# A decode attention kernel: TensorE's loop step reordered to keys, last chunk, maximum, values, with the last chunk of the last pair ahead of the values of the pair before it

## The chip, the cores and the metric

The kernel runs on one core of one Trainium2 chip. The metric is the device time of one execution in microseconds (us). Before the change three runs gave 1269.72, 1269.49 and 1268.3 us, so the median is 1269.49 us. The profiled execution, from which all durations below come, took 1268.6 us, and its span from the first to the last instruction is 1266.8 us.

## The reference

One new token is attended against a cache of 65,536 positions, and the result is mixed with a small token MLP. The parts that matter:

```python
q = (x @ wq)                     # 16 query heads of 256, 8 key/value heads, so 2 query heads per cache head
scores = einsum("bhqd,bhkd->bhqk", q, k) * (Dh ** -0.5)     # k_cache: 8 x 65536 x 256 bf16
p = softmax(scores, axis=-1)
a = einsum("bhqk,bhkd->bhqd", p, v).reshape(1, 1, 4096) @ wo   # v_cache: 8 x 65536 x 256 bf16
b = mixer(layernorm(x), w1, b1, w2, b2)                     # gelu, 1792 wide
return g * a + (1 - g) * b                                  # g = sigmoid(sum(x * gate_w))
```

Both caches are read once, 537 MB together; everything else is small.

## The kernel before

**Tiling.** A cache head has 65,536 positions. A *chunk* is 2,048 positions (16 tiles of 128), a *pair* is 8 chunks (`BODY = 8`), so a pair of one cache is 8.39 MB. There are 32 pairs (`NP = 32`), four to a head (`PPH = 4`). Pairs and chunks count from 0 here; the argument of `values(v)` counts from 1, so `values(31)` works on pair 30.

**What is done to a pair.** For each chunk TensorE transposes 16 key tiles into PSUM (`transposes`, L335, the matmuls at L348), VectorE and ScalarE copy them to SBUF (`ktT<-kst`, L681 and L821), and TensorE multiplies them with the head's two queries (`scores`, L360, the matmuls at L369). A chunk's scores are issued one step behind its transposes. `keys` (L375) does the transposes of chunks 0 to 6 and the scores of chunks 0 to 5; `last_keys` (L382) does the transposes of chunk 7 and the scores of chunks 6 and 7. Then the running maximum is updated: VectorE reduces the scores (L687, L690), TensorE transposes the result (L390), VectorE reduces again (L692, L694), TensorE broadcasts it (L392), VectorE rescales the accumulators (L697 to L710, semaphore `s_acc`), ScalarE forms the weights `pT`. `values` (L408) then sums the denominators (L397) and multiplies `pT` with the 128 value tiles in `vbuf` (L404).

**Buffers.** `kring` holds one and a half pairs of keys, `vbuf` one pair of values.

**The DMA order.** All large loads stand on SyncE's (SP's) queue in a fixed order (L283 to L316). The load of key pair j waits until TensorE has transposed chunk 3 of pair j-1 (L288, `sem_tr`). The load of value pair j waits until the values of pair j-1 are done (L276, `sem_pv`). The last value pair, pair 31, comes in five pieces (L68, L305): tiles 0 to 47 go into `kring` once all keys of pair 30 are transposed; tiles 48 to 95, 96 to 111, 112 to 123 and 124 to 127 go into `vbuf` and wait for `sem_pv` 31, that is for the values of pair 30. The last two loads of the projection weights `wo` (L314) stand behind them.

**TensorE's loop.** The order of work on TensorE is made at run time: a loop of 35 passes (L540) over parts guarded by conditions on register counters. `k_reg`, `l_reg` and `v_reg` count the pairs whose keys, last chunk and values have been issued. In each pass come `keys` (if `k < cap`), `values` (if `v < l`), then in one condition (`l < k`) the last chunk, the head's end (`clear`, `by_row`, `project`), the mixer's product, `maxima` and, for the last pair, `first_of_last` (L424), and at the very end `tail` (L477). Followed by hand, the registers give: pairs 0 and 1 run keys, last chunk, maximum, values one pair after the other; pair 2 stops after its maximum; from pair 3 on the order is keys j, values j-1, last chunk j, maximum j. The order at the end is keys 31, values of pair 30, last chunk 31, maximum 31, `first_of_last` (the first 48 value tiles of pair 31), the rest of its values, `tail`.

**The wait `s_qc`.** VectorE copies the two queries of the next head into `qcur` after the maximum of the head's last pair (L744, L767) and increments `s_qc`; TensorE waits for it ahead of each pair's keys (L546).

**The end.** `first_of_last` waits for `s_acc`, for the weights and for `s_mix` (VectorE's L771 to L774). `values(32)` waits for the pieces of tiles 48 to 95 and 96 to 111. `tail` waits for VectorE's copy of the accumulators (`accs`, L715), transposes them (L452), adds the last 16 tiles (L445), waits for VectorE's `oTn` (L728) and projects with `wo` (L471).

Of the kernel before, what the change touches and what calls it, by code (L numbers as in the profile page):

```python
# [12 lines left out]
def bass_gated_mix__gqa_block_cached__mixer_token_mlp__decode_kernel(  # L13
# [17 lines left out]
    H = A_k_cache.shape[1]  # L31
# [4 lines left out]
    REP = HQ // H  # L36
# [59 lines left out]
    with ctx:  # L96
# [6 lines left out]
        def new_sem(name):  # L103
            return ctx.enter_context(nc.semaphore(name))
# [91 lines left out]
        sem_k = new_sem("sem_k")  # L196
        sem_kb = new_sem("sem_kb")
        sem_kc = [new_sem("sem_kc%d" % i) for i in range(3)]
        s_qc = new_sem("s_qc")
        sem_v = new_sem("sem_v")  # L200
        sem_vp = [new_sem("semvp%d" % i) for i in range(len(pieces))]
        sem_x = new_sem("sem_x")
# [128 lines left out]
        def _(pe):  # L331
# [3 lines left out]
            def transposes(k, c, j, u16, x2):  # L335
                if k == 0:
                    pe.wait_ge(sem_k, u16)
                if k == DC:
                    pe.wait_ge(sem_kb, 16)
                    for p, sem in zip((LEAD, LEAD + 1, NP - 1), sem_kc):  # L340
                        with pe.If(j == p):
                            pe.wait_ge(sem, 16)

                def tiles(at):
                    for b in range(NB):
                        pe.wait_ge(sem_ev[b], c + 1)
                        for i in range(4):
                            ins = pe.transpose(kst[:, b, i * P:(i + 1) * P],  # L348
                                               kring_f[:, at + NT * (k % DC) + 4 * b + i, :], ident[:, :])
                        ins.then_inc(sem_tr[b], 1)  # L350

                if k < DC:
                    tiles(HV)
                else:
                    with pe.If(x2 == 0):
                        tiles(0)
                    with pe.Else():
                        tiles(NV)
# [16 lines left out]
            def keys(c0, j, *where):  # L375
                j1 = pe.snap(j + 1, min_val=1, max_val=NP)
                transposes(0, c0, j, *where)
                for k in range(1, BODY - 1):
                    transposes(k, c0 + k, j, *where)
                    scores(k - 1, c0 + k - 1, j1)  # L380
# [19 lines left out]
            def some(n0, n1, buf):  # L400
                for n in range(n0, n1):
                    r, nt = divmod(n, NT)
                    o = 32 * (n % 4)
                    ins = pe.matmul(acc[o:o + REP, 0:DH], pT[:, r, 2 * nt:2 * nt + 2], buf[:, n, :],  # L404
                                    start=False, stop=False, skip_group_check=True)
                return ins

            def values(v):  # L408
                pe.wait_ge(s_acc, v)
                pe.wait_ge(sem_exp, pe.snap(v + 1, min_val=2, max_val=NP + 1))  # L410
                denominators()
                with pe.If(v < NP):
                    pe.wait_ge(sem_v, pe.snap(v * 16, min_val=16, max_val=16 * NP))
                    some(0, NRING, vbuf)
                for n0, n1 in pieces[1:]:
                    if n0 < NLATE:
                        with pe.If(v == NP):
                            piece_wait(n0)
                        ins = some(n0, n1, vbuf)
                ins.then_inc(s_early, 1)  # L420
                with pe.If(v < NP):
                    some(NLATE, NV, vbuf).then_inc(sem_pv, 1)

            def first_of_last():  # L424
                pe.wait_ge(s_acc, NP)
# [94 lines left out]
            def reg(name, value):  # L520
                r = pe.alloc_register(name)
                pe.reg_mov(r, value)
                return r
# [3 lines left out]
            k_reg = reg("k_reg", 0)  # L527
            l_reg = reg("l_reg", 0)
            v_reg = reg("v_reg", 0)
            cap_reg = reg("cap_reg", 1)  # L530
            mk_reg = reg("mk_reg", 0)
            gk_reg = reg("gk_reg", 1)
            mv_reg = reg("mv_reg", 0)
            gv_reg = reg("gv_reg", 1)
            mix_reg = reg("mix_reg", 1)
            def val(r, lo=0, hi=NP):
                return pe.snap(r, min_val=lo, max_val=hi)

            on = OrderedEngineSet([pe.engine])
            with nc.Fori(0, NP + LEAD + 1, 1, engines=on, head_slot={pe.engine: 0}):  # L540
                with pe.If(val(k_reg) < val(cap_reg)):
                    j = pe.snap(k_reg, min_val=0, max_val=NP - 1)
                    with pe.If(val(mk_reg) == PPH):
                        pe.reg_mov(mk_reg, 0)
                        pe.reg_add(gk_reg, gk_reg, 1)
                    pe.wait_ge(s_qc, pe.snap(gk_reg, min_val=1, max_val=H))  # L546
                    keys(pe.snap(j * BODY, min_val=0, max_val=NC), j,
                         pe.snap(j * 16 + 16, min_val=16, max_val=16 * NP),
                         pe.snap(x2_reg, min_val=0, max_val=NV))
                    pe.reg_sub(x2_reg, NV, x2_reg)  # L550
                    pe.reg_add(k_reg, k_reg, 1)
                    pe.reg_add(mk_reg, mk_reg, 1)
                with pe.If(val(v_reg) < val(l_reg)):
                    pe.reg_add(v_reg, v_reg, 1)
                    pe.reg_add(mv_reg, mv_reg, 1)
                    pe.reg_add(cap_reg, v_reg, 1)
                    v = pe.snap(v_reg, min_val=1, max_val=NP)
                    values(v)
                    with pe.If(v >= LEAD):
                        pe.reg_mov(cap_reg, NP)  # L560
                with pe.If(val(l_reg) < val(k_reg)):
                    l = pe.snap(l_reg, min_val=0, max_val=NP - 1)
                    last_keys(pe.snap(l * BODY, min_val=0, max_val=NC), pe.snap(x2l_reg, min_val=0, max_val=NV))
                    pe.reg_sub(x2l_reg, NV, x2l_reg)
                    with pe.If(val(mv_reg) == PPH):
                        pe.reg_mov(mv_reg, 0)
                        g1 = pe.snap(gv_reg, min_val=1, max_val=H)
                        pe.wait_ge(s_cp, g1)
                        clear(acc[:, 0:NACC])
                        by_row(acc[:, SELC:NACC]).then_inc(s_sel, 1)  # L570
                        pe.wait_ge(sem_wo, pe.snap(g1 * 16, min_val=16, max_val=16 * H))
                        pe.wait_ge(s_oTn, g1)
                        project(range(2 * REP)).then_inc(s_proj, 1)
                        pe.reg_add(gv_reg, gv_reg, 1)
                    with pe.If(l > MIX0):
                        with pe.If(l < MIX0 + FT + 1):
                            pe.wait_ge(s_pb, val(mix_reg, 1, FT))
                            pe.reg_add(mix_reg, mix_reg, 1)
                            for q in range(NCG):
                                pe.matmul(prj[32 * q:32 * q + 1, WG:2 * WG], w2cur[:, :],  # L580
                                          gu[:, q * WG:(q + 1) * WG], start=False, stop=True, skip_group_check=True)
                    pe.reg_add(l_reg, l_reg, 1)
                    maxima(pe.snap(l_reg, min_val=1, max_val=NP))
                    with pe.If(val(l_reg) == NP):
                        first_of_last()
                with pe.If(val(v_reg) == NP):
                    tail()

        @block.vector
        def _(vec):  # L590
# [150 lines left out]
            vec.wait_ge(s_q, 1)  # L741
            vec.tensor_copy(qT[:, :, :].rearrange("p a b -> p (a b)"), sps[:, 1, 0:2 * HQ])
            vec.drain()
            vec.tensor_copy(qcur[:, :, :], qT[:, :, 0:REP]).then_inc(s_qc, 1)  # L744
            vec.wait_ge(s_h, 1)
            vec.drain()
            vec.tensor_copy(bcast[:, :], prj[:, DM:DM + 3])
# [5 lines left out]
            with nc.Fori(0, H, 1, engines=on) as g:  # L753
                with nc.Fori(0, PPH, 1, engines=on) as m:
                    j = vec.snap(g * PPH + m, min_val=0, max_val=NP)
                    c0 = vec.snap(j * BODY, min_val=0, max_val=NC)
                    for k in range(BODY):
                        evacuate(k, c0 + k)
                    with vec.If(j > 0):
                        with vec.If(m < 1):  # L760
                            finish_head(g)
                    maxima(vec.snap(j + 1, min_val=1, max_val=NP), c0)
                    with vec.If(j >= MIX0):
                        with vec.If(j < MIX0 + FT):
                            mixer(vec.snap(kt_reg, min_val=0, max_val=FT - 1))
                with vec.If(g < H - 1):
                    vec.tensor_copy(qcur[:, :, :], qT[:, :, bass.ds(vec.snap(q_reg, min_val=REP, max_val=HQ - REP), REP)]  # L767
                                    ).then_inc(s_qc, 1)
                    vec.reg_add(q_reg, q_reg, REP)
            vec.wait_ge(s_proj, H - 1)  # L770
            vec.tensor_copy(brow1, prj[:, WG:2 * WG])  # L771
# [88 lines left out]
```

## Time and profile before

| quantity | before |
|---|---|
| median of three runs | 1269.49 us (1268.3 to 1269.72) |
| the profiled execution | 1268.6 us |
| its span | 1266.8 us |
| data read | 544.22 MB, 430 GB/s over the span |
| busy: TensorE matmul, ScalarE, VectorE | 922.7, 544.0, 497.1 us |
| mean granted TensorE clock | 0.841 |
| DMA queue of the large loads | 99.6% of 16 engines' span |

How to read it: a pair of keys and a pair of values are 16.8 MB, and in the middle of the run one such couple lands every 38.7 us. TensorE's work on a couple is shorter, so it waits once per pair for keys. An engine's busy share is an average over all stages, and the first 100 us and the last 30 us are built differently from the middle.

### The profile page before, as it was taken

Reading aid. Unit: us, or ns where it says so; the run is one execution under the profiler, and the core shown is the slowest. Engines: PE = TensorE matmul, PEld = TensorE weight load, DVE = VectorE, ACT = ScalarE, POOL = GpSimd, SP = SyncE. Lnnn points to the kernel's source line nnn. Section 1 sums busy time; section 2 is a strip of 40 time slices with the busy share of each in tenths; the row PEclk is TensorE's granted clock in tenths of the full one; section 3 lists DMA queues with packets and bytes.
Section 4 is the critical chain, followed back from the end, with each engine's and each line's share of the span. In section 5 each row is a group of like instructions: output and inputs, shape, how many; then the busy total and the mean of one; then the engine's idle time right before and its main releaser. Section 6 shows DMA issues by size and latency. Waiting matters only on the chain.

```text
span 1266.8 us, 40261 instructions
## 1 busy us (share of the span) xinstructions
PE 922.7 (73%) x17201; PEld 867.2 (68%) x17201; DVE 497.1 (39%) x1125; ACT 544.0 (43%) x692; POOL 0.9 (0%) x7
## 2 busy tenths in 40 slices
PE   4588877678676687766887667876669766688685
PEld 3577866578676687665777566875668766687684
DVE  3233444343443444544445333333334332343341
ACT  2354543344433454443544334443444443354451
POOL 0000000000000000000000000000000000000000
PEclk9798887789777898778888789877789877898787
DMA  9999999999999999999999999999999999999998
GB/s 416 432 396 430 447 430 430 441 435 430 430 430 443 432 430 430 430 443 432 430 430 436 437 432 430 430 437 437 432 430 430 437 435 435 430 430 430 427 434 346
DMA packets 12054, 544.37 MB, mean 430 GB/s; under 512 B 1417, under 2 KB 1676, under 8 KB 2956
## 3 DMA queue, kind: packets, MB, share of 16 engines
q1 hardware_dynamic: 11954, 544.22, 99.6%
q8 instruction: 7, 0.11, 0.0%
q10 hardware_dynamic: 90, 0.01, 0.0%
q14 instruction: 3, 0.02, 0.0%
HBM read 544.22 MB, written 0.00 MB: 430 GB/s over the span
## 4 chain that ended last, share of the span: by engine, by line
DMA 68%; PE 30%; issue 1%; DVE 0%; SPq 0%; DVEq 0%
DMA kring<-in_A_k_cache_dram 65%; PE kst L348 24%; PE sps L369 5%; DMA vbuf<-in_A_v_cache_dram 3%; PE acc L404 2%; PE acc L397 0%; PE sps L392 0%; DVE mcol L687 0%; PE sps L445 0%; PE sps L452 0%; DVE acc L710 0%; PE sps L390 0%; DVE mrow L692 0%; DVE accs L715 0%; DVE mdiag L694 0%
## 5 line engine op out<-in xcount | busy, mean ns | idle before, releaser
L348 PE MATMUL kst<-ident,kring 128*128 128x128 f32 x4096 | 555.5, 296 | 266.8 <-DMA kring<-in_A_k_cache_dram 233.5
L821 ACT ACTIVATE ktT<-kst 128x1024 bf16<-128x1024 bf16 x512 | 498.5, 1021 | 539.9 <-PE kst L348 539.5
L348 PEld LDWEIGHTS kst<-ident,kring 128*128 128x128 f32 x4096 | 504.7, 154 | 281.3 <-issue 280.6
L681 DVE COPY ktT<-kst 128x1024 bf16<-128x1024 bf16 x512 | 354.2, 692 | 636.0 <-PE kst L348 612.1
L369 PEld LDWEIGHTS sps<-qcur,ktT 128*128 128x128 bf16 x8192 | 238.1, 96 | 2.6
L369 PE MATMUL sps<-qcur,ktT 128*128 128x2 bf16 x8192 | 236.7, 163 | 0.0
L404 PE MATMUL acc<-vbuf,pT 128*2 128x256 bf16 x4032 | 122.1, 282 | 5.9 <-DMA vbuf<-in_A_v_cache_dram 5.6
L404 PEld LDWEIGHTS acc<-vbuf,pT 128*2 128x2 bf16 x4032 | 94.3, 86 | 25.5 <-DMA vbuf<-in_A_v_cache_dram 5.7
L804 ACT ACTIVATE fade<-mdif 128x2 f32<-128x2 f32 x32 | 6.5, 203 | 112.0 <-DVE mdif L698 112.0
L392 PEld LDWEIGHTS sps<-mdiag,mones 2*128 2x128 f32 x64 | 13.0, 252 | 28.4 <-DVE mdiag L694 28.4
L392 PE MATMUL sps<-mdiag,mones 2*128 2x2 f32 x64 | 15.8, 313 | 21.3 <-DVE mdiag L694 21.3
L808 ACT ACTIVATE pT<-sps,mneg 128x64 f32 x128 | 30.4, 334 | 0.0
L826 ACT ACTIVATE z_b<-z_b 128x448 bf16<-128x448 bf16 x14 | 8.1, 576 | 48.1 <-DVE z_b L668 48.1
L687 DVE TENSOR_REDUCE mcol<-sps 128x2 f32<-128x256 f32 x32 | 13.5, 422 | 33.6 <-PE sps L369 33.6
L390 PE MATMUL sps<-ident,mcol 128*2 128x128 f32 x32 | 9.7, 302 | 12.9 <-DVE mcol L690 10.5
L397 PE MATMUL acc<-pT,ones_sq 128*128 128x32 bf16 x256 | 11.7, 179 | 7.7 <-DVE acc L710 3.4
L710 DVE TENSOR_SCALAR acc<-acc,fader 128x256 f32<-128x256 f32 x32 | 15.8, 493 | 2.5
L397 PEld LDWEIGHTS acc<-pT,ones_sq 128*128 128x128 bf16 x256 | 8.6, 97 | 10.8 <-issue 7.2
L692 DVE TENSOR_REDUCE mrow<-sps 2x1 f32<-2x128 f32 x32 | 8.9, 279 | 15.9 <-PE sps L390 15.9
L390 PEld LDWEIGHTS sps<-ident,mcol 128*2 128x2 f32 x32 | 2.6, 80 | 16.2 <-DVE mcol L690 12.6
L697 DVE TENSOR_SCALAR mneg<-sps 128x2 f32<-128x2 f32 x32 | 5.1, 159 | 18.7 <-PE sps L392 18.7
L460 PEld LDWEIGHTS acc<-sel,accs 128*64 128x64 f32 x112 | 10.8, 214 | 0.9
(108 smaller groups left out, 163.4 us busy)
## 6 DMA issues: line engine op xcount, KB each, us to landing
kring<-in_A_k_cache_dram SPq DMA_DIRECT2D x8, 4096.0 KB, 24.3
wo_sb<-in_A_wo_dram SPq DMA_DIRECT2D x7, 448.0 KB, 28.6
vbuf<-in_A_wq_dram SPq DMA_DIRECT2D x1, 3072.0 KB, 10.3
kring<-in_A_v_cache_dram SPq DMA_DIRECT2D x1, 3072.0 KB, 38.8
vbuf<-in_A_v_cache_dram SPq DMA_DIRECT2D x1, 3072.0 KB, 9.6
vbuf<-in_A_v_cache_dram SPq DMA_DIRECT2D x1, 1024.0 KB, 11.6
vbuf<-in_A_v_cache_dram SPq DMA_DIRECT2D x1, 768.0 KB, 13.1
vbuf<-in_A_wq_dram SPq DMA_DIRECT2D x1, 512.0 KB, 11.1
```

The source lines that it names most:

```text
L348: ins = pe.transpose(kst[:, b, i * P:(i + 1) * P], kring_f[:, at + NT * (k % DC) + 4 * b + i, :], ident[:, :])
L369: ins = pe.matmul(sps[:, 0, 2 * (NT * k + nt):2 * (NT * k + nt) + 2], ktT[:, par, b, ntl * DH + dj:(ntl + 1) * DH:2], qcur[:, dj, :], star ...
L390: pe.transpose(mxT, mcol[:, :], ident[:, :]).then_inc(s_mT, 1)
L392: pe.matmul(mxB, mones[:, :], mdiag[:, :], start=True, stop=True).then_inc(s_mB, 1)
L397: pe.matmul(acc[:, DENC:SELC], ones_sq[:, :], pT[:, r, :], start=False, stop=(r == BODY - 1), skip_group_check=True)
L404: ins = pe.matmul(acc[o:o + REP, 0:DH], pT[:, r, 2 * nt:2 * nt + 2], buf[:, n, :], start=False, stop=False, skip_group_check=True)
L460: ins = pe.matmul(dst[hh * HP:(hh + 1) * HP, i:i + 1], accs[:, i:DH:2 * REP], sel[:, hh:hh + 1], start=False, stop=True, skip_group_check= ...
L681: vec.tensor_copy(ktT[:, k % KTB, b, :], kst_b[:, b, :]).then_inc(sem_ev[b], 1)
L687: vec.tensor_reduce(out=mcol[:, :], in_=scores_all.rearrange("p (n hh) -> p hh n", hh=REP), axis=AX.X, op=ALU.max)
L710: vec.tensor_scalar(acc[:, 0:DENC], acc[:, 0:DENC], fader[:, :], None, op0=ALU.mult).then_inc(s_acc, 1)
L808: ins = act.activation(pT[:, bass.ds(p0, DC), hh:2 * NT:REP], scores_all.rearrange("p (a r n hh) -> p a hh r n", a=2, r=DC, hh=REP)[:, hal ...
L821: act.activation(ktT[:, k % KTB, b, :], kst_b[:, b, :], AF.Copy).then_inc(sem_ev[b], 1)
```

## The change

Lines left out of the diff are the calls of `keys` and `last_keys` with their arguments, and the head's end and the mixer's product, which are as before. The loop body is cut into four conditions, in the order keys, last chunk, maximum, values, and the loop has 61 passes (`2 * NP - LEAD - 1`). Two registers say what may go: `lcap_reg` (how far the last chunk may run ahead) and `need_reg` (how many pairs' keys must be issued before the next values).

```diff
-            with nc.Fori(0, NP + LEAD + 1, 1, engines=on, head_slot={pe.engine: 0}):
-                with pe.If(val(k_reg) < val(cap_reg)):
...
-                    pe.wait_ge(s_qc, pe.snap(gk_reg, min_val=1, max_val=H))
...
+            with nc.Fori(0, 2 * NP - LEAD - 1, 1, engines=on, head_slot={pe.engine: 0}):
+                with pe.If(val(k_reg) < NP):
+                    with pe.If(val(l_reg) == val(k_reg)):
...
+                        pe.reg_add(k_reg, k_reg, 1)
+                        with pe.If(val(k_reg) == NP):
+                            pe.reg_mov(lcap_reg, NP)
                 with pe.If(val(l_reg) < val(k_reg)):
+                    with pe.If(val(l_reg) <= val(lcap_reg)):
...
+                        pe.reg_add(l_reg, l_reg, 1)
+                with pe.If(val(m_reg) < val(l_reg)):
+                    with pe.If(val(v_reg) == val(m_reg)):
...
+                        pe.reg_add(m_reg, m_reg, 1)
+                        maxima(pe.snap(m_reg, min_val=1, max_val=NP))
+                        with pe.If(val(m_reg) == NP):
+                            first_of_last()
+                with pe.If(val(v_reg) < val(m_reg)):
+                    with pe.If(val(k_reg) >= val(need_reg)):
+                        pe.reg_add(v_reg, v_reg, 1)
+                        pe.reg_add(mv_reg, mv_reg, 1)
+                        v = pe.snap(v_reg, min_val=1, max_val=NP)
+                        pe.reg_mov(lcap_reg, v)
+                        with pe.If(v >= LEAD):
+                            pe.reg_add(need_reg, v_reg, 2)
+                        with pe.If(v == NP - 1):
+                            pe.reg_mov(need_reg, NP)
+                        values(v)
```

Besides, the semaphore `s_qc`, its wait and the two registers for it are gone (the copies into `qcur` stay), `tail()` moves into the `Else` of the last condition of `values`, and the bound `c + 1` in `transposes` is taken once as `done`.

Followed by hand, the registers of the changed loop give the same order of work as before for pairs 0 to 30, with one pass for keys and values and another for the last chunk and the maximum from pair 3 on. The end differs: keys 31, last chunk 31, values of pair 30, maximum 31, `first_of_last`, the rest. In the program's text the last chunk now stands ahead of the maximum, and the maximum ahead of the values; before, the values stood between keys and last chunk. Counted in the built programs, TensorE's loop body grows from 1,531 to 1,542 instructions of 64 bytes; it begins on a boundary of 256 instructions in both.

## The prediction

> **What bounds the kernel now.** I read the page's parts on DMA first, then windows, then TensorE and SyncE in order of time at both ends of the run.
>
> ```profile
> DMA  9999999999999999999999999999999999999998
> q1 hardware_dynamic: 11954, 544.22, 99.6%
> q8 instruction: 7, 0.11, 0.0%
> ```
>
> The large loads fill the span, so time can only be won where the queue runs dry. The windows (last column GB/s, the one before it DMA share) find two such places:
>
> ```profile
> 70.00:75.00 5.00, 3.10 (x50) 2.66 (x39) 1.39 (x2) 1.26 (x2) 0.00 (x0) 1.00 0.89 328
> 200.00:1200.00 1000.00, 728.56 (x13568) 689.36 (x13569) 401.56 (x906) 434.98 (x554) 0.00 (x0) 0.83 1.00 434
> 1247.50:1250.00 2.50, 2.43 (x42) 2.13 (x31) 1.17 (x2) 0.86 (x1) 0.00 (x0) 1.00 0.63 187
> ```
>
> 434 GB/s is the full rate: over those 1,000 us nothing is to be had. SyncE's issues that end the two dips:
>
> ```profile
> 70.71 0.33 SPq L265 DMA_DIRECT2D vbuf<-in_A_v_cache_dram  x1
> 1247.94 1.85 SPq L265 DMA_DIRECT2D vbuf<-in_A_v_cache_dram  x4
> 1249.84 0.95 SPq L314 DMA_DIRECT2D wo_sb<-in_A_wo_dram  x2
> ```
>
> The first is value pair 1, waiting for the values of pair 0; the second the late pieces of pair 31, waiting for the values of pair 30. TensorE at the start, then at the end (start, us, work, idle before):
>
> ```profile
> 43.15 0.94 PE L369 MATMUL sps<-qcur,ktT 128*128 128x2 bf16 x32
> 53.60 3.67 PE L348 MATMUL kst<-ident,kring 128*128 128x128 f32 x16 [9.51 <-issue]
> 61.26 0.37 PE L390 MATMUL sps<-ident,mcol 128*2 128x128 f32 x1 [2.30 <-issue]
> 64.92 5.74 PE L404 MATMUL acc<-vbuf,pT 128*2 128x256 bf16 x128
> ...
> 1235.82 0.36 PE L397 MATMUL acc<-pT,ones_sq 128*128 128x32 bf16 x8
> 1241.79 6.09 PE L404 MATMUL acc<-vbuf,pT 128*2 128x256 bf16 x128 [5.61 <-DMA vbuf<-in_A_v_cache_dram]
> 1247.96 1.96 PE L348 MATMUL kst<-ident,kring 128*128 128x128 f32 x16
> 1249.75 1.74 PE L369 MATMUL sps<-qcur,ktT 128*128 128x2 bf16 x64
> 1252.25 0.27 PE L390 MATMUL sps<-ident,mcol 128*2 128x128 f32 x1 [0.76 <-DVE mcol L690]
> 1256.46 2.73 PE L404 MATMUL acc<-kring,pT 128*2 128x256 bf16 x48
> 1259.79 2.23 PE L404 MATMUL acc<-vbuf,pT 128*2 128x256 bf16 x64 [0.27 <-issue]
> 1264.27 0.37 PE L471 MATMUL prj<-wo_sb,oTn 128*1 128x112 bf16 x16 [0.25 <-DVE oTn L728]
> ```
>
> At 1236.2 TensorE stands still for 5.6 us until value pair 30 has landed (1241.75); the last chunk of pair 31, whose keys landed at 1222.4, waits behind those values although nothing but order holds it.
>
> **The change, part by part.** The sum stands against the profiled execution, 1268.6 us; the median of the three runs, 1269.49, is 0.9 above it, so I carry the difference over.
>
> *Last chunk of pair 31 ahead.* Its 3.53 us of matmuls (1247.96 to 1251.49) move into the 5.6 us hole: keys end at 1235.7, the chunk would end near 1239.7, 2.1 us before the values can start. It brings a wait: its last scores wait for the copies of chunk 7 by VectorE and ScalarE, with the values of pair 30 queued behind; the 2.1 us cover that, and if pair 30 landed earlier the loss would be at most 3.5 us of delay to the pieces' issue. VectorE's reduction (L687, L690) is then done too, so 1247.9 to 1252.25, 4.3 us, leave TensorE's chain. Of SyncE's queue nothing changes place; the four pieces and the two `wo` loads behind them still wait for the values of pair 30.
>
> Next late are these loads. By the trace's landing records the pieces came at 1249.0, 1257.5, 1260.0, 1261.9 and 1262.5, the halves of `wo` at 1263.1 and 1263.7. If they stay there, the second half of L471 starts at about 1263.75, takes 0.2 us, and ends 0.7 us before the present 1264.67: a gain of 0.7. They come earlier if the values of pair 30 end earlier. The dip cost 2.5 x (1 - 187/434) = 1.4 us. At the full clock the same 128 matmuls take 3.66 us (1164.99, pair 28) instead of 6.09; then the values end at 1245.45, the pieces are queued before the one in `kring` is through (1248.3), and the dip is gone. Tiles 48 to 95 land at 1256.1, their 48 matmuls at the half clock (2.7, the row of 1256.46) end at 1258.8, 16 more at 1259.8, and from there to the end of L471 took 2.65 us (1262.02 to 1264.67): 1262.5, gain 2.2; with L452 and L445 at the half clock too, 1.8.
>
> So the gain is 0.7 to 2.2, and the clock decides. The hole shrinks from 5.6 to 2.1 us.
>
> ```profile
> 1209.27:1212.68 3.41, 2.66 (x74) 2.51 (x72) 1.71 (x4) 1.94 (x2) 0.00 (x0) 1.00 0.92 396
> 1212.68:1215.50 2.82, 0.73 (x3) 0.50 (x3) 1.62 (x9) 1.06 (x5) 0.00 (x0) 0.50 1.09 465
> ```
>
> The column ahead of the DMA share is the granted clock. It fell to 0.50 at 1212.68 with no TensorE gap over 0.8 us, only one transposing burst and two-column scores before it. The last chunk leaves just that before the values, so they may still start at half clock and recover sooner. I take the middle, 1.3. The Trainium skill, "TensorE: Matmul & The Clock Gate", section "Why this matters for your kernels", asks for no idle gap over some 3 us to keep the clock; by that alone the values would run at the full clock and the gain would be 2.2 instead of 1.3. The row of 1212.68 speaks against relying on it.
>
> *Program text.* At the start TensorE waits for its own code: 9.51 us ahead of the first last chunk, 2.30 ahead of the first maximum, while seven code packets of 16,384 bytes start at 18.3, 24.5, 36.4, 43.7, 50.7, 58.3 and 65.4. Last chunk 0 begins in the fifth packet of the loop before (instruction 1,061 of the body; a packet of 16,384 bytes holds 256), in the third and fourth now (743). The fourth starts at 43.7 and, by the 2.9 us from 50.7 to 53.6, is usable at 46.6 rather than 53.6. Maximum 0 (1,023) then waits for the fifth until about 54, the values of pair 0 (1,155 on, crossing into the sixth at 1,280) until about 61.6, and end near 64 instead of 70.7. Key pair 1 ends at 72.4, so value pair 1 is then queued 6 us ahead and joins without a gap. It landed 20.25 us after key pair 1 (72.42 to 92.67); a load in the middle takes 19.35 (half of 38.70). Gain 0.9; none if a code packet is 7 us later than I think, and a loss of about 1 if two are. From there on all loads run one behind the other, so what is won stays won.
>
> *Conditions.* One more turn of the loop and some skipped conditions per pair: not separate rows, but L348 after a maximum shows 1.43 us of "issue" at 1215.5, a whole loop turn with the end of the maximum in it, so under 2 us a pair. TensorE idles 9.4 us a pair for keys (1183.74), and a key load lands 28.0 us after its issue for 19.35 us of transfer, 8.65 us in hand. Cost nothing; without that cover 2 x 29 = 58 us.
>
> *`s_qc` gone.* Seven times the first transposes of a head no longer wait for VectorE's copy; the keys land later anyway. Nothing, on the same cover. `done` and the place of `tail`: nothing.
>
> Sum: 1268.6 - 0.9 - 1.3 = 1266.4 for a profiled execution, 1267.3 as a median.
>
> **Rivals.**
>
> *Nothing is won.* The values still take about 6 us because the clock falls in the new hole, and value pair 1 is no earlier because code comes later. For it: the row of 1212.68. Against it: the 0.7 us of the chain hold at any clock. Time 1268.8 to 1269.8.
>
> *The loop no longer stays in instruction memory: slower.* The body grows from 1,531 to 1,542 instructions, past 1,536, so the back branch lies in a seventh packet. For it: the growth over exactly that edge, and 61 turns instead of 35. Against it: seven packets were fetched and none after 65.4 us, so six of the loop and the one behind it stay. Price: one packet refetched a turn, about 7.5 us with two turns a pair, 15.0 against 8.65 us in hand: 6.35 x 29 = 184 us, 1454 us. It decides from more than 8.65 us of refetching a pair on; one packet a pair would cost nothing. The Trainium skill, "Runtime: NRT & Kernel Launch", section "Instruction fetch mechanics", says only two lines are held and a branch out of them is fetched anew; by that the kernel before would have fetched in every turn, and the trace shows none.
>
> *Order not as stated.* Followed by hand, the registers give last chunk 31 ahead of the values of pair 30 (`lcap` becomes 32 when `k` does), so I give it 0.01 of the first rival's chance, and its time.
>
> **How the numbers follow.** Forecast 0.79, nothing won 0.14, code refetched 0.07. Within the forecast the gain runs from 0.7 (one part) to 3.1 (0.9 and 2.2). 0.2%, about what a measurement of this kernel can tell from no change, is 2.5 us, which needs both parts with most of the clock's share, or a median on the lucky side of the 1.4 us spread seen before: I give 0.41 of the 0.79 to that. Faster 0.41; same 0.38 + 0.11 = 0.49; slower 0.07 + 0.03 = 0.10. The range takes 3.1 us and 0.5 of spread below, and nothing won with 0.4 of spread above: 1265.9 to 1269.9.
>
> **What would show it.** Right: SyncE issues value pair 1 near 65 and it lands 19.4 us after key pair 1; L348 of the last chunk starts near 1236 and the values of pair 30 right when their data lands; the dip at 1247.5 is smaller and the pieces land up to 1.4 us sooner relative to value pair 30; L390 follows the values by under 1 us. Wrong: instruction packets after the first 80 us; couples further apart than 38.7 us; values of pair 30 of 6 us or more; value pair 1 issued after 70 us.

## The result: 38 us slower, and the profile after

Six runs of the changed kernel gave a median of 1307.3 us (1303.51 to 1311.66), six of the kernel before 1269.24 (1268.3 to 1270.12): 1.0298 times the time, with a 95% interval of 1.0275 to 1.0322. The profiled execution took 1303.66 us, its span is 1301.8 us against 1266.8, so there are 35.0 us to find. First the page of the changed kernel: span, GB/s in 40 slices, two DMA queues, the shares of the chain that ended last, and two groups of TensorE (busy, mean ns, idle before and what ended it).

```profile
span 1301.8 us, 41027 instructions
...
GB/s 414 425 427 438 427 437 432 432 429 417 411 369 419 419 419 387 419 369 417 415 391 439 350 419 439 429 421 433 447 423 447 432 424 443 425 441 429 427 443 306
...
q1 hardware_dynamic: 11954, 544.22, 97.5%
q8 instruction: 8, 0.13, 0.0%
...
PE 55%; DMA 27%; issue 10%; DVE 6%; DVEq 1%; ACT 1%; SPq 0%
...
L349 PE MATMUL kst<-ident,kring 128*128 128x128 f32 x4096 | 585.6, 305 | 164.2 <-issue 82.7
...
L398 PE MATMUL acc<-pT,ones_sq 128*128 128x32 bf16 x256 | 11.8, 181 | 66.3 <-issue 62.9
```

The queue of the large loads was full for 99.6% of the span and is now at 97.5%. GB/s is below 420 in all but one of slices 10 to 24, that is from 293 to 781 us, and back at the old level after that. The chain, 68% DMA and 30% TensorE before, is now 55% TensorE, and 10% is "issue", time in which TensorE waited for nothing that the profile shows. Two groups say where: 62.9 us ahead of the denominators (L398; before, the same group waited 7.7 us in all, 0.5 of it for issue), 82.7 us ahead of the transposes (L349; 32.0 before).

The landing records of the loads divide the 35.0 us. The start won 0.7: value pair 1 landed at 91.97 instead of 92.67. Between the landings of value pairs 1 and 30 the time grew from 1149.1 us to 1183.1, so 34.0 were lost there; pairs 5 to 20 hold all of it, with key pairs 39 to 46 us apart instead of 38.7. The end, from the landing of value pair 30 to the end of the span, took 26.7 us instead of 25.05: 1.7 lost.

Now the middle, one pair in each kernel. TensorE before, in order of time (start, us, work, idle before it and who ended that):

```profile
385.99 3.67 PE L404 MATMUL acc<-vbuf,pT 128*2 128x256 bf16 x128
389.72 1.96 PE L348 MATMUL kst<-ident,kring 128*128 128x128 f32 x16
391.52 1.74 PE L369 MATMUL sps<-qcur,ktT 128*128 128x2 bf16 x64
393.83 0.22 PE L580 MATMUL prj<-gu,w2cur 128*1 128x112 bf16 x4 [0.57 <-issue]
...
405.19 6.30 PE L348 MATMUL kst<-ident,kring 128*128 128x128 f32 x32 [9.87 <-DMA kring<-in_A_k_cache_dram]
```

And the same stretch after:

```profile
402.88 0.36 PE L398 MATMUL acc<-pT,ones_sq 128*128 128x32 bf16 x8 [2.19 <-issue]
403.17 3.66 PE L405 MATMUL acc<-vbuf,pT 128*2 128x256 bf16 x128
408.07 1.96 PE L349 MATMUL kst<-ident,kring 128*128 128x128 f32 x16 [1.24 <-issue]
409.87 1.74 PE L370 MATMUL sps<-qcur,ktT 128*128 128x2 bf16 x64
413.10 0.22 PE L577 MATMUL prj<-gu,w2cur 128*1 128x112 bf16 x4 [1.48 <-issue]
...
416.22 3.67 PE L349 MATMUL kst<-ident,kring 128*128 128x128 f32 x16 [1.66 <-issue]
421.78 3.67 PE L349 MATMUL kst<-ident,kring 128*128 128x128 f32 x16 [1.89 <-DVE ktT L687]
```

Between keys and values, values and last chunk, last chunk and mixer's product stand 2.19, 1.24 and 1.48 us of "issue" where there were none, none and 0.57. The wait of 9.87 us for keys is gone; instead the transposes of chunk 1 wait for VectorE's copy of chunk 0 (L687). VectorE in the changed kernel shows why:

```profile
415.66 0.49 DVE L716 TENSOR_SCALAR acc<-acc,fader 128x256 f32<-128x256 f32 x1
416.34 0.34 DVE L662 TENSOR_SCALAR wtmp<-hbT,params 128x448 bf16<-128x448 bf16 x1 [0.19 <-issue]
...
420.32 0.39 DVE L680 TENSOR_TENSOR gu<-wtmp,z_b 128x448 bf16<-128x448 bf16 x1
421.04 1.29 DVE L687 COPY ktT<-kst 128x1024 bf16<-128x1024 bf16 x2 [0.33 <-issue]
```

Behind the maximum it rescales the accumulators (L716) and then, in pairs 4 to 17 only, computes a tile of the mixer (L662 to L680), until 6.1 us after the end of TensorE's last maximum matmul (414.57 to 420.71). Before, the same lay inside TensorE's wait for keys:

```profile
401.08 0.39 DVE L674 TENSOR_TENSOR gu<-wtmp,z_b 128x448 bf16<-128x448 bf16 x1
406.41 0.69 DVE L681 COPY ktT<-kst 128x1024 bf16<-128x1024 bf16 x1 [4.93 <-PE kst L348]
```

VectorE was idle for 4.93 us there. That, rather than TensorE's 9.87, was the cover; and behind the ends of heads, where the maximum comes later, it was only 0.65 to 1.99 us. The tightest place is behind the maximum of pair 8 (the same view of before):

```profile
365.54 0.39 DVE L674 TENSOR_TENSOR gu<-wtmp,z_b 128x448 bf16<-128x448 bf16 x1
366.58 0.69 DVE L681 COPY ktT<-kst 128x1024 bf16<-128x1024 bf16 x1 [0.65 <-PE kst L348]
```

At last the granted clock in the changed kernel (the column ahead of the DMA share): the values of pair 9, then the transposes behind the maximum of pair 10.

```profile
442.00:446.00 4.00, 3.98 (x84) 2.89 (x88) 0.00 (x0) 0.00 (x0) 0.00 (x0) 0.58 1.17 508
455.00:458.70 3.70, 2.25 (x10) 2.17 (x11) 2.36 (x10) 1.06 (x5) 0.00 (x0) 0.50 0.82 354
```

At that clock sixteen transposes take up to 3.67 us (416.22) instead of 1.96, and the 128 value matmuls at 442.31 take 5.33 instead of 3.67.

### The profile page after: what moved, and what is told of

Its sections match the earlier page's. It is cut to its first block, busy times and chain, and to the rows that moved or that the text cites. A ratio compares the mean times of both kernels' runs of the same rounds, so it can differ in the third digit from the quotient of the medians.

```text
span 1301.8 us, 41027 instructions
## 1 busy us (share of the span) xinstructions
PE 978.6 (75%) x17201; PEld 903.0 (69%) x17201; DVE 495.8 (38%) x1125; ACT 544.9 (42%) x692; POOL 0.9 (0%) x7
## 3 DMA queue, kind: packets, MB, share of 16 engines
q1 hardware_dynamic: 11954, 544.22, 97.5%
## 4 chain that ended last, share of the span: by engine, by line
PE 55%; DMA 27%; issue 10%; DVE 6%; DVEq 1%; ACT 1%; SPq 0%
PE kst L349 33%; DMA kring<-in_A_k_cache_dram 25%; PE sps L370 11%; PE acc L405 7%; DMA wo_sb<-in_A_wo_dram 1%; PE sps L393 1%; DVE ktT L687 1%; ACT z_b L832 1%; PE acc L463 1%; PE acc L398 1%; PE sps L391 0%; DVE mrow L698 0%; DVE z_b L668 0%; DVE wtmp L666 0%; DVE z_b L672 0%
## 5 line engine op out<-in xcount | busy, mean ns | idle before, releaser
L349 PE MATMUL kst<-ident,kring 128*128 128x128 f32 x4096 | 585.6, 305 | 164.2 <-issue 82.7
L349 PEld LDWEIGHTS kst<-ident,kring 128*128 128x128 f32 x4096 | 527.2, 159 | 184.1 <-issue 148.9
L687 DVE COPY ktT<-kst 128x1024 bf16<-128x1024 bf16 x512 | 352.9, 691 | 636.5 <-PE kst L349 608.8
L405 PE MATMUL acc<-vbuf,pT 128*2 128x256 bf16 x4032 | 146.5, 315 | 1.8 <-DMA vbuf<-in_A_v_cache_dram 1.3
L405 PEld LDWEIGHTS acc<-vbuf,pT 128*2 128x2 bf16 x4032 | 105.1, 96 | 34.9 <-issue 2.7
L398 PE MATMUL acc<-pT,ones_sq 128*128 128x32 bf16 x256 | 11.8, 181 | 66.3 <-issue 62.9
L398 PEld LDWEIGHTS acc<-pT,ones_sq 128*128 128x128 bf16 x256 | 8.7, 98 | 69.3 <-issue 65.7
L391 PE MATMUL sps<-ident,mcol 128*2 128x128 f32 x32 | 10.1, 314 | 25.5 <-DVE mcol L696 18.3
L716 DVE TENSOR_SCALAR acc<-acc,fader 128x256 f32<-128x256 f32 x32 | 15.8, 493 | 2.5
L577 PE MATMUL prj<-gu,w2cur 128*1 128x112 bf16 x56 | 3.4, 234 | 17.1 <-issue 17.1
```

The costliest lines, as they stand in the source:

```text
L349: ins = pe.transpose(kst[:, b, i * P:(i + 1) * P], kring_f[:, at + NT * (k % DC) + 4 * b + i, :], ident[:, :])
L398: pe.matmul(acc[:, DENC:SELC], ones_sq[:, :], pT[:, r, :], start=False, stop=(r == BODY - 1), skip_group_check=True)
L687: vec.tensor_copy(ktT[:, k % KTB, b, :], kst_b[:, b, :]).then_inc(sem_ev[b], 1)
L716: vec.tensor_scalar(acc[:, 0:DENC], acc[:, 0:DENC], fader[:, :], None, op0=ALU.mult).then_inc(s_acc, 1)
```

## The experiments

Theory A, formed from these rows: the conditions cost TensorE's sequencer over 4 us a pair; in pairs 4 to 17 that pushes the next keys against VectorE's mixer; the extra standing halves the clock; the three together bring a pair over the 38.7 us of its loads. Rivals: B, the conditions and the half clock alone, in whatever pair; C, the new order at the end; D, the missing wait `s_qc` or the second pass of the loop; E, the mixer's load on VectorE wherever it stands, or TensorE's product with its wait. All times are medians; "before", run again beside each of them, was 1269.2 to 1269.9. One table for all, as means over pairs 6 to 18 from the traces: from the first transposes to the last maximum matmul, and how much of it had the half clock. It leaves out the wait for keys; heads are in it. The time from a maximum to the next keys, 1.4 us at the least, comes on top; the loads of a couple take 38.7 us, called the beat below.

| kernel | time | ratio (95%) | keys to maximum, us | half clock, us |
|---|---|---|---|---|
| before | 1269.2 | | 30.5 | 5.1 |
| changed | 1307.3 | 1.0298 (1.0275 to 1.0322) | 40.2 | 13.7 |
| 1 changed, no mixer | 1273.28 | 1.0029 (1.0016 to 1.0041) | 35.7 | 8.3 |
| 2 before, no mixer | 1270.01 | 1.0002 (0.9992 to 1.0012) | 30.4 | 4.8 |
| 3 before, 12 conditions more | 1333.77 | 1.0497 (1.0479 to 1.0515) | 39.1 | 11.2 |
| 4 before, only the end's order | 1272.35 | 1.0021 (1.0010 to 1.0033) | 31.7 | 6.1 |
| 5 changed, mixer spread | 1271.01 | 1.0010 (1.0001 to 1.0019) | 35.1 | 6.7 |
| 6 changed, `s_qc` back | 1307.34 | 1.0281 (1.0263 to 1.0299) | 38.6 | 13.4 |
| 7 before, 6 conditions more | 1295.19 | 1.0185 (1.0167 to 1.0204) | 37.4 | 12.9 |
| 8 lean | 1269.02 | 0.9998 (0.9989 to 1.0007) | 32.1 | 5.6 |
| 9 changed, filler | 1301.57 | 1.0271 (1.0238 to 1.0304) | 38.2 | 7.1 |
| 10 lean, filler | 1270.64 | 1.0003 (0.9994 to 1.0012) | 32.1 | 4.4 |
| 11 lean, filler, tail outside | 1267.72 | 0.9987 (0.9977 to 0.9996) | 32.1 | 4.6 |

**1 and 2: the mixer left out.** In both kernels VectorE's, ScalarE's and TensorE's mixer work of pairs 4 to 17 is left out; every condition on TensorE stays.

```diff
-                    with vec.If(j >= MIX0):
-                        with vec.If(j < MIX0 + FT):
-                            mixer(vec.snap(kt_reg, min_val=0, max_val=FT - 1))
```

> The changed kernel with the mixer of pairs 4 to 17 left out on VectorE, ScalarE and TensorE (the MLP's product is left out; TensorE's conditions stay). Theory A (TensorE's sequencer needs about 4 us more a pair for the conditions, which keys waited for before, and only where VectorE's 5 us of mixer stand right behind the maximum does TensorE become the bound): the couples of pairs 5 to 19 land every 38.7 us as in the rest, 1266 to 1271 us, some 35 below the changed kernel. Rival B (the conditions and the half clock alone cost it, in whatever pair): still over 1290. Rival C (the last chunk's new place at the end costs it): still over 1290.

> The control: the kernel before with the same mixer work left out. All theories: the mixer lies beside TensorE's 9 us wait for keys, so nothing changes, 1267 to 1270 us. If it falls by much, e1 says nothing.

34 of the 38 us are gone, and in pairs 5 to 20 key pairs are as far apart as before: B and C are refuted as main causes. So is the second pass of D, for all 61 are still there. 1273.28 lies 2.3 us above A's range; what is left is lost at the end, where keys 31 start 8.3 us after their landing, so that the values of pair 30 start 6.4 us after their landing. The control shows that the mixer costs the kernel before nothing.

**5: the mixer spread.** The mixer's operations are put two or three at a time behind VectorE's copies of chunks 0, 1, 2, 3 and 5 of the next pair, and ScalarE's tanh behind its copy of chunk 4. TensorE's program is untouched.

```diff
+                        mixer(k, j)
...
-                    with vec.If(j >= MIX0):
-                        with vec.If(j < MIX0 + FT):
-                            mixer(vec.snap(kt_reg, min_val=0, max_val=FT - 1))
```

> The changed kernel with the mixer's ten operations on VectorE spread between the copies of chunks 0 to 5 of the following pair (ScalarE's tanh after its copy of chunk 4), instead of standing in one piece behind the maximum; TensorE's stream is untouched. Theory A (conditions and a mixer that blocks the copies of chunk 0 together): chunk 1 follows chunk 0 in 3.5 us also in pairs 5 to 18, couples land every 38.7 us, 1268 to 1276 us. Rival E (what counts is the mixer's load on VectorE, wherever it stands, or TensorE's product with its wait): still over 1290.

1271.01, with all the work, all 61 passes and all conditions in place. TensorE in its trace, the maximum of one pair and the next keys:

```profile
397.99 0.22 PE L577 MATMUL prj<-gu,w2cur 128*1 128x112 bf16 x4 [1.34 <-issue]
...
404.73 6.30 PE L349 MATMUL kst<-ident,kring 128*128 128x128 f32 x32 [5.28 <-DMA kring<-in_A_k_cache_dram]
```

The issue gaps are still there (1.34), yet TensorE waits 5.28 us for keys again, and chunk 1 follows chunk 0 without a gap. The place of the mixer on VectorE, met by the late TensorE, is what made the loss in the middle. Rival E falls as well. With VectorE out of the way the conditions cost nothing there; at the end they still do: from the landing of value pair 30 to the end of the span it is 30.9 us here and 31.7 without the mixer, against 25.05 before, though the start is 0.6 to 0.9 us earlier.

**3 and 7: conditions added to the kernel before.** Conditions that are never true are added around keys, values and last chunk: 12 a pair (6, 3, 3), then 6 (3, 2, 1), which is about half of what the change adds.

```diff
+                def pad(n):
+                    for _ in range(n):
+                        with pe.If(val(k_reg) < val(pad_reg)):
+                            pe.reg_mov(pad_reg, 0)
```

> The kernel before, its order, end and number of loop turns untouched, with 12 conditions that are never true put on TensorE in each pair: 6 between keys and values, 3 between values and last chunk, 3 between last chunk and maximum, about 0.35 us each, 4.2 us a pair. Theory A: the loss comes back without the changed order: 1290 to 1315 us, the couples of pairs 5 to 19 at 39.5 us or more and one near 46 after some heads' ends. Rival C (the new order at the end) and rival D (the wait s_qc taken away, or the second turn of the loop): 1268 to 1272.

> The kernel before with 6 conditions never true in each pair (3, 2, 1 at the three places), 2.1 us. Theory A, which has a threshold: of the 9.4 us wait for keys 7.3 are left, more than the 6.4 us from the maximum to the mixer's end, so the middle keeps 38.7 us a couple; only the heads 8, 12, 16 (5.6 us in hand, and s_qc) lose a few us, and the start 5 to 9 us because the loop's back branch lies in the seventh code packet: 1273 to 1287. If the loss goes with the number of conditions: half of what 12 cost, about 1300.

Both missed theory A's range, on the high side: 64.5 and 25.5 us lost, and the second lies nearer to the other reading in its expectation, that the loss goes with the number of conditions (about 1300). The order of work, `s_qc` and the 35 passes are those of before, so conditions do it without any of them: C and D fall. In both, value pair 1 comes late at the start (8.9 and 5.3 us), a cost of another kind: the loop is longer than six code packets of 256 instructions, so its last branch lies in a seventh. With six conditions the span grew by 27.0 us: 10.3 up to key pair 5 (the late value pair 1 and its sequel), 13.9 from key pair 5 to 19, 0.5 from there to key pair 31, 2.3 behind it. Some 2.1 us a pair should have stayed under the threshold and did not. TensorE after the end of a head, in pair 5 of that kernel:

```profile
217.33 0.58 PE L392 MATMUL sps<-mdiag,mones 2*128 2x2 f32 x2 [0.66 <-DVE mdiag L704]
219.73 3.67 PE L348 MATMUL kst<-ident,kring 128*128 128x128 f32 x16 [1.82 <-DMA kring<-in_A_k_cache_dram]
225.16 3.07 PE L348 MATMUL kst<-ident,kring 128*128 128x128 f32 x14 [1.76 <-DVE ktT L691]
```

Behind a head's end VectorE had 0.65 to 1.99 us in hand and not 4.93, so the collision with the mixer can begin there with far less than 4 us. But TensorE also comes late from the start (key pair 5 lands 10.3 us later than before), and no run here separates the two. From then on TensorE stays late, with 12.9 us of half clock a pair instead of 5.1, until the mixer has done its last tile (on time from pair 19 on). A late start alone does not do it: value pair 1 comes 5.2 and 5.6 us late in kernels 4 and 10 too, and they lose nothing in the middle.

**4: the end's order alone.** Before, with a second copy of the last chunk inside the keys' condition for pair 31, and the maximum in a condition of its own.

```diff
+                    with pe.If(val(k_reg) == NP):
+                        last_keys(pe.snap(val(l_reg, 0, NP - 1) * BODY, min_val=0, max_val=NC), ...)
+                        pe.reg_add(l_reg, l_reg, 1)
...
+                with pe.If(val(m_reg) < val(l_reg)):
```

> The kernel before with only the last chunk of pair 31 put ahead of the values of pair 30 (a copy of its code inside the keys' condition, the maximum in a condition of its own), so under 1 us of conditions more a pair; the wait s_qc stays. Theory A: no loss in the middle, 1266.5 to 1269.5 us; the values of pair 30 start when their data land, and the end is 0.7 to 2 us shorter than before. Rival C: the end is longer, over 1271; if the loss sat in the order it is over 1290.

TensorE at both ends in its trace:

```profile
69.45 0.39 PE L397 MATMUL acc<-pT,ones_sq 128*128 128x32 bf16 x8 [4.73 <-issue]
...
1241.81 1.96 PE L348 MATMUL kst<-ident,kring 128*128 128x128 f32 x16 [0.29 <-issue]
...
1246.83 3.67 PE L404 MATMUL acc<-vbuf,pT 128*2 128x256 bf16 x128 [0.86 <-DMA vbuf<-in_A_v_cache_dram]
```

The last chunk lies in the hole, the values start 0.04 us after their data (1246.79) at the full clock, and the end takes 23.75 us instead of 25.05: 1.3 won. The kernel misses its range (1266.5 to 1269.5) and is slower all the same, because value pair 1 lands 5.2 us later. The second copy of the last chunk makes the loop some 200 instructions longer; code arrives later for the last chunk already, and ahead of the values of pair 0 stand 4.73 us of "issue". The end of the loop lies in the seventh packet, whose fetch began at 65.25 us, and the branch at 64.23 us that jumps over `first_of_last` to there lasts 3.49 us instead of 0.2.

**6: `s_qc` back.**

> The changed kernel with the wait s_qc put back ahead of the keys. Theory A: the wait now ends only behind the mixer of the head's last pair (pairs 7, 11, 15), as in the kernel with 12 conditions, where keys 8 began 6.6 us after the maximum: 4 to 6 us more at three heads and what follows from it, 1310 to 1330 us. Rival D (taking the wait away is what costs): under 1295.

Missed: 1307.34, no change. At heads TensorE starts keys 9.6 to 9.8 us after their landing, waiting for VectorE's copy of the queries behind the mixer, and then no longer waits at chunk 1. The wait only changes its place; taking `s_qc` out was worth nothing.

**8: the lean version.** The changed kernel's order of work with one pass a pair: text order keys, values, last chunk, maximum, one register (`vl_reg`) that holds the values of pair 30 back, and a guard on the maximum.

```diff
-                with pe.If(val(v_reg) < val(l_reg)):
+                with pe.If(val(v_reg) < val(vl_reg)):
...
+                    with pe.If(val(k_reg) == NP):
+                        pe.reg_mov(vl_reg, 0)
...
+                with pe.If(val(m_reg) < val(l_reg)):
+                    with pe.If(val(v_reg) == val(m_reg)):
```

> The changed kernel's order of work, last chunk of pair 31 ahead of the values of pair 30 included and s_qc gone, but in one turn a pair as before: text order keys, values, last chunk, maximum, with a register that holds the values of pair 30 back, 1,534 instructions in the loop, so the back branch stays in the sixth packet. Theory A: no loss in the middle, none at the start, and the end 1.3 us shorter as in e4: 1266.5 to 1269 us. Rival: if the new order itself costs, over 1272.

1269.02, nothing lost in the middle: it runs 24 conditional branches a pair on TensorE where before has 22 and the changed kernel 36. Behind heads' ends VectorE has nothing in hand here either (its copy of chunk 0 follows the mixer after 0.33 us in pairs 5, 9, 13 and 17), but chunk 1 still follows chunk 0 in 3.46 us or less. So VectorE may come a little late without holding TensorE up, and a collision that small does not spread. The 1.3 us at the end that were expected are not won: TensorE waits 2.01 us for conditions ahead of the values of pair 30, and they run at the half clock:

```profile
1243.11 0.36 PE L396 MATMUL acc<-pT,ones_sq 128*128 128x32 bf16 x8 [2.01 <-issue]
1243.41 5.33 PE L403 MATMUL acc<-vbuf,pT 128*2 128x256 bf16 x128
```

**9 and 10: filler against the half clock.** Matmuls whose results nobody reads, put where TensorE would stand still; most of them start new sums in `prj`'s bank, and the result changes in these two.

```diff
+                for _ in range(12):
+                    pe.matmul(prj[:, 2 * P:4 * P], ones_sq[:, :],
+                              ones_sq[:, :].rearrange("p (o n) -> p o n", o=1).broadcast_to((P, 2, P)),
+                              start=True, stop=True, skip_group_check=True)
```

> The changed kernel with idle-time filler on TensorE: 5 and 12 matmuls (128x256, bf16, results never read) behind the two instructions of the maximum, 12 behind the transposes of chunk 0, so that TensorE has work where it waits for conditions and for VectorE. Theory A with the half clock as its amplifier: the filler lies in waits of 0.7, 1.7 and 2 us and costs little; the half clock, 12 to 15 us a pair in pairs 5 to 18, falls below 6, chunks 0 and 1 take 2 us instead of 3.7, keys to maximum fall from 39 to 42 us to 35 to 38, under the 38.7 of the loads, and the time to 1272 to 1285. Theory A without the clock (conditions and the wait for VectorE alone are enough): keys to maximum stay above 38.7 and the time at 1298 or more. In between the clock carries a share, read from the time lost in pairs 5 to 20 (35.2 us in the changed kernel).

> The lean version (same order at the end, one turn a pair) with 14 matmuls (128x256, bf16, results never read) behind the last chunk of each pair, so that TensorE does not stand still ahead of the values of pair 30. If idling ahead of the values is what halves the clock there: the values of pair 30 take 3.7 us instead of 5.33, the pieces are issued 1.6 us earlier, the stretch from the landing of value pair 30 to the end of the span falls from 25.2 to about 23.6, and the time to about 1267.4, 0.9985 of before. If the filler brings the clock down itself or delays the values: 1269 or more. The middle should stay at 38.7 us a pair.

The first missed A's range: 1301.57, which by the expectation speaks for conditions and the wait for VectorE being enough without the clock. Its runs go from 1287.51 to 1309.95, and the profiled one is the lowest. In that one key pairs 5 to 20 took 601.0 us, 585.1 in the kernel before: 15.9 lost instead of 34.0, with the half clock down from 13.7 to 7.1 us a pair. Pairs 6 and 7 had 1.5 us of it and ran from keys to maximum in 35.0 us, at a beat of 38.7, although all conditions were there and chunk 1 still came 4.8 to 5.0 us after chunk 0. So conditions and that wait alone can leave a pair inside its beat. Of the pairs 6 to 18 the five with under 4 us of half clock took 34.9 to 36.7 us, the other eight, with 9.2 us and more, 38.1 to 42.4. How large the clock's share is in a typical run stays open, since the filler itself takes time and did not always hold the clock. In the lean version the values of pair 30 took 3.67 us and the end 23.9 us, as expected, but the time was not: 1270.64. Value pair 1 landed at 98.23, a seventh packet again, by 28 more instructions.

**11: the lean version with filler, and `tail` outside the loop.** The lean version with the filler (`start=False`, so nothing is overwritten), and `tail` behind the loop, which takes 102 instructions out of it.

```diff
-                with pe.Else():
-                    tail()
...
+            tail()
```

> The lean version with 14 fillers behind each last chunk, and the last piece's tail behind the loop instead of in it, which shortens the loop to about 1,450 instructions, so that its branch back lies in the sixth code packet again. If the 5.2 us at the start of the version with fillers came from the branch back lying in the seventh packet, value pair 1 lands at 93 or before instead of 98.2; with the end as there (23.9 us from the landing of value pair 30 to the end of the span, 25.05 in the kernel before) the span is 1265.5 to 1266.5 and the time 1267.2 to 1268.6, ratio about 0.999. If the loss at the start has another cause: 1270 or more. If the code behind the loop comes late at the end: the end grows by the 3 to 7 us that such a packet takes, 1271 or more.

1267.72 us, 0.9987 of before: 0.13% less, with an interval that stays just under 1. TensorE around the values of pair 30, then SyncE's issue of the late pieces:

```profile
1240.38 1.74 PE L368 MATMUL sps<-qcur,ktT 128*128 128x2 bf16 x64
1241.98 1.69 PE L386 MATMUL prj<-ones_sq 128*128 128x256 bf16 x14
1244.25 0.36 PE L399 MATMUL acc<-pT,ones_sq 128*128 128x32 bf16 x8 [0.58 <-issue]
1244.54 3.66 PE L406 MATMUL acc<-vbuf,pT 128*2 128x256 bf16 x128
```

```profile
1248.25 2.32 SPq L264 DMA_DIRECT2D vbuf<-in_A_v_cache_dram  x4
```

Value pair 30 landed at 1243.53 and the span ended at 1267.1: 23.6 us, 1.5 less than before. Value pair 1 landed at 94.39, not "at 93 or before" and 1.7 us later than before, and the profiled span missed its expected bounds by 0.6; the time and the ratio did not. So the trace shows a better end and a worse start, in a span no shorter than the 1266.8 us of before; that the kernel is faster rests on the medians of 11 and 15 runs alone.

## Why the prediction was wrong

**The failing step is "Conditions", in its size and, above all, in its cover.** Size: "under 2 us a pair" was read from the one gap behind a maximum. That row holds the turn of the loop and nothing of the conditions between the parts. Measured in the changed kernel's records of TensorE's sequencer, a pair has 36 conditional branches (22 before); one that is taken lasts 169 to 219 ns, mostly 207, one that is not about 75 ns, each with a register operation of mostly 30 to 50 ns ahead of it. In the gaps that is 2.19 us, 1.24 less none, 1.48 less 0.57: 4.3 us a pair, and 4.1 in other pairs. The Trainium skill, "Advanced Engine Details and Errata", section "Control Flow Timing", gives about 108 ns for a compare-and-branch; the trace shows one value below that and one at twice it.

Cover: "TensorE idles 9.4 us a pair for keys ... Cost nothing". The 9.4 us were right for the pair they were read from; behind heads' ends it is 5.6 to 6.9 us. The fallback, "without that cover 2 x 29 = 58 us", came nearer to the 35 us. TensorE's wait was cover for someone else as well: VectorE's rescaling and mixer ran in it until 401.47, and VectorE was free for 4.93 us, after heads' ends for 0.65 to 1.99. The runs split the 9.7 us from 30.5 to 40.2. With the mixer left out or spread (1 and 5), the same conditions bring keys to maximum to 35.7 and 35.1 us: 4.6 to 5.2 us, which the wait for keys still covers, so that TensorE stands on average 3.2 and 3.8 us between a maximum and the next keys (8.5 before). But the mixer ends 6.1 us behind the maximum. With it in its place TensorE stands for VectorE, 5.6 to 6.4 us pass from the start of chunk 0 to that of chunk 1 instead of 3.46, and the half clock grows from 6.7 to 8.3 us a pair to 13.7; together that is the other 4.5 to 5.1 us, over the 38.7 of the loads. How those divide between the wait and the clock is not shown: half of the added half clock, 2.7 to 3.5 us, is the most that the clock can have. The row that decides this stood in the profile of the kernel before, the idle time ahead of L681, and the prediction does not use it.

**The clock.** The prediction leaned on the row in which the clock fell to 0.50 with no gap over 0.8 us, and that held: in the changed kernel it halves again and again in pairs 5 to 18, where no gap of TensorE is over 3.0 us and most are 0.7 to 2.2. By the rule of the Trainium skill that the prediction cites ("TensorE: Matmul & The Clock Gate", section "Why this matters for your kernels"), to leave no idle gap of over some 3 us, it would have stayed at full speed there; the trace does not bear this out. The prediction applied the row to the end alone and not to the middle, where its own conditions made new gaps.

**Program text: right.** SyncE issued value pair 1 at 65.6 us, "near 65". It landed 19.35 us after key pair 1, the figure forecast, and 0.7 us earlier than before, for 0.9 predicted.

**The last chunk of pair 31: right in direction, not in this kernel.** Predicted 1.3, and 1.3 in the kernel that changes the end alone. That the two agree is partly luck: there the values of pair 30 ran at the full clock (3.67 us), for which the sum gave 1.8 to 2.2, and in the lean version, where they started 1.4 us after their landing and took 5.33, the end was 0.1 longer, where 0.7 less was to "hold at any clock". In the changed kernel TensorE was late. Its end, TensorE and then SyncE:

```profile
1252.13 5.12 PE L349 MATMUL kst<-ident,kring 128*128 128x128 f32 x32 [1.65 <-issue]
...
1272.66 1.96 PE L349 MATMUL kst<-ident,kring 128*128 128x128 f32 x16 [0.87 <-issue]
...
1277.84 0.36 PE L398 MATMUL acc<-pT,ones_sq 128*128 128x32 bf16 x8 [1.64 <-issue]
1278.14 5.33 PE L405 MATMUL acc<-vbuf,pT 128*2 128x256 bf16 x128
```

```profile
1283.51 1.85 SPq L264 DMA_DIRECT2D vbuf<-in_A_v_cache_dram  x4
```

Key pair 31 had landed at 1246.0 and its transposes begin 6.1 us later; in pair 31 the keys come only 29.1 us after those of pair 30, while it took TensorE 33.4 us to get from those of pair 30 to its maximum (1217.1 to 1250.5), so any condition there makes it later. Value pair 30 landed at 1275.07, its matmuls start 2.8 us later and at the half clock, and the pieces are issued 8.4 us after the landing instead of 6.2. Hence 1.7 lost instead of 1.3 won.

**`s_qc`, order, code.** `s_qc` was worth nothing, as predicted, though not because of "the same cover". The order was as stated. The rival of refetched code did not happen: eight code packets, none after 76.2 us, in 61 passes. The price of a seventh packet is paid once, at the start, in kernels whose branch back is needed early. What did happen, TensorE and VectorE colliding behind the maximum, was not among the rivals.

## What to carry to other kernels

A wait on the busiest engine is cover for every engine that works during it: before spending it, read how long each of the others is idle at the end of it, in the tightest pair and not in the mean one. A condition in a run-time loop is work of the engine's sequencer; count the taken and untaken branches of a pass and price them. Where a beat has little left, ask also what more standing does to the clock: here the pairs that were late were those with more half clock too, though no run shows how much of the loss is the clock's.

## What was not expected of the hardware

A taken conditional branch on TensorE's sequencer took mostly 207 ns and an untaken one about 75 ns, so in these kernels skipping a part costs its condition more than entering it. Six never-true conditions a pair, some 2.1 us, cost 25.5 us in all, 5.3 of them at the start, with half-clock stretches of 12.9 us a pair instead of 5.1. In four kernels the end of the loop lies in the seventh code packet and the values of pair 0 come in the second pass; value pair 1 landed 5.2 to 5.6 us late in three (4, 7 and 10) and 8.9 in the fourth (3), and a branch at the end of the first pass lasted 2.6 to 5.8 us there. The changed kernel, whose values stand at the end of the first pass, paid nothing. Fourteen matmuls without use, 1.69 us, ahead of the values of pair 30 came with 3.66 us for these instead of 5.33 (11 against 8); ahead of the values of pair 0 the same fourteen took 3.10 us and the values 5.33.
